# One load of matrices asked for a block later, and the first block of each hop closed six pairs later, in a seven-hop graph kernel

## The chip, the cores and the metric

The kernel runs on one core of a Trainium2 chip. The metric is the device time of one execution in microseconds. Three runs of the kernel before took 3917.54, 3921.28 and 3921.52 us; their median is 3921.28 us. The engines are named as in the profile: PE is TensorE's matmul pipe and PEld its weight loads, DVE is VectorE, ACT is ScalarE, POOL is GpSimd and SP is SyncE, which here only issues DMA. A suffix q (SPq, POOLq, ACTq) names the same engine's queue of DMA issues and waits.

## The reference

A graph of 10,000 nodes and 160,000 edges has a row of 128 numbers for each node. Seven times in a row each node's new row is the weighted sum of the rows of the nodes with an edge into it; the eight versions of a node (the input and seven hops) are then the tokens of a small attention block.

```python
h = x
toks = [x]
for _ in range(K):                                  # K = 7
    msg = h[src] * deg_inv_sqrt[src, None] * deg_inv_sqrt[dst, None]
    h = _segment_sum(msg, dst, N)
    toks.append(h)
tok = jnp.stack(toks, axis=1)                       # (N, K+1, D)
t = _layernorm(tok, axis=-1)
...
o = tok + jnp.einsum('nkd,de->nke', o, wo)
r = _layernorm(o, axis=-1)
alpha = _softmax(jnp.einsum('nkd,d->nk', r, w_r), axis=-1)
return jnp.einsum('nk,nkd->nd', alpha, o)
```

A hop needs all rows of the hop before it: an edge may come from any node. That is why the border between two hops, called a seam here, is a place where work can run dry.

## The kernel before, in words

The nodes are cut into 79 blocks of 128 rows; 78 of them go through the main path. A hop's rows are kept twice: as a table in SBUF (`tab`, fp16 in a high and a low half, so 256 columns) and as a table in DRAM (`tabd`, and its last seven blocks once more as `tabh`). Edges were sorted once, in the first stage, into 0/1 matrices (`gsd` in DRAM), 592 KB for each block of targets. In the hops 2 to 7 such a block, `block()`, does this:

- `gather(jj)`, nine times, one for each pair of edge groups: eight matmuls (L635) pick source rows out of the SBUF table into the PSUM tile `p` (six buffers), and ACT or DVE copies `p` to `eb` (L638; pairs with jj % 3 = 1 go to DVE). All 72 matmuls of a block's nine gathers stand in a row on PE.
- `begin()`: opens the accumulator `acc` (PSUM, two buffers) with rows that were fetched from DRAM by indirect DMA into `og`: one matmul for the rows from `tabh` (L599, `og,w`), and one for the overflow rows from `tabd` (L599, `og,Sov`).
- `scat(jj)`, nine times: two matmuls for each pair (L613) add the rows of `eb` into `acc`.
- `close()`: ends the sum. In the first two blocks of a hop (`late`) the overflow rows are added only here (L626), and not in `begin()`, because the DMA that fetches them must wait until the last rows of the hop before have been stored to `tabd`. Then `finish()` reduces `acc` to `s` on DVE (L585), `next_rows()` scales `s` into the next table (three DVE instructions, L665 to L667, in all hops but the last) and stores it to `tabd` (L162), and `token_out()` writes the hop's rows out (POOL L675, SP L677).

The list `pend` carries `scat` and `close` behind `gather`: after the nine gathers of a block, all but the last two entries of `pend` are run. So PE sees, for block n: 72 gather matmuls of n, `begin` of n, the last two pairs of n-1 (four matmuls), the `close` of n-1, and the first seven pairs of n (14 matmuls). At the end of a hop the list is emptied.

The overflow rows of the first five blocks of a hop are asked for by `over()`, issued on POOL from `ahead()`: for block 0 while block 0 gathers, for the blocks 1 and 2 while block 1 gathers, for 3 and 4 while block 2 gathers. Those issues are POOL's L559, each behind a small copy (L569) that ties it to a point of the gathers. In the seam of the hops 2 to 6, the scale of the next table is worked out as well (`scale`, a short chain of DVE and two tiny PE steps, L129 and L137).

The 0/1 matrices of a block come by a load on SP's queue (`load_w`, L760, tile `w`, five buffers): at each block the list `ws` of loaded blocks is filled up to four. A load waits until PE has done with the buffer that it reuses.

What sets the order: the code is written in the order told above, but a scheduler between the code and the chip places the instructions on each engine's queue. Where a line of code stands is therefore not where its instruction stands; the order of the built program is shown with the change. Each engine runs its own queue in order.

In names below, "block 0" is the first block that a hop works on (the blocks held in `tabh` go first), "block 1" the second, and T is the time at which the overflow rows of block 0 are there and PE goes on.

Of the kernel before, what the change touches and what calls it, by code (L numbers as in the profile page):

```python
# [40 lines left out]
class Hops:  # L41
    def __init__(self, ctx, dp, missing, tab1, tc, x, src, dst, dis):
# [68 lines left out]
        self.Sov = cp.tile([128, NW + NE, 128], F8, name="Sov")  # L111
        self.oidx = cp.tile([128, NW + NE, NI + 1], I32, name="oidx")
        self.ebuf = []
        self.eb_i = 0
        self.more_ebufs(cp, 5, True)

# [471 lines left out]
    def block(self, t, w, tab, og, pend, lag, runs, first, evac, fin, lead=False, late=False, mid=None, ahead=None):  # L588
# [8 lines left out]
        def fetched(i, start=False, stop=False):  # L597
            W = w[:, (NG + i) * 128:(NG + i + 1) * 128] if i < NI else self.Sov[:, t, :]
            T.matmul(acc[0][:, :256], W, og()[i], start=start, stop=stop)  # L599
            if first:  # L600
                T.matmul(acc[0][:, 256:257], W, self.ones16, start=False, stop=False)

        def begin():
            acc.append(self.pacc.tile([128, 512], F32, name="acc", tag="acc"))
            for i in range(NI if late else NI + 1):
                fetched(i, start=i == 0)
# [22 lines left out]
        def gather(jj):  # L629
            n = min(2, NG - 2 * jj)  # L630
            p = self.pg.tile([128, 2, 2, 128], F32, name="p")
            for j in range(n):
                for q in range(4):
                    s = 4 * (2 * jj + j) + q
                    T.matmul(p[32 * q:32 * q + 32, j], w[:, NJ * 128 + s * CAP:NJ * 128 + (s + 1) * CAP], tab[:, s, :], start=True, stop=True)  # L635
            e = self.ebuf[self.eb_i % len(self.ebuf)]
            self.eb_i += 1
            (A.copy if evac(jj) else V.tensor_copy)(e[:, :n, 0:256], p[:, :n].rearrange("p j h d -> p j (h d)"))  # L638
            pend.append(lambda: scat(e[:, :n], jj))

        jj = 0
        for i, n in enumerate(runs):
            for _ in range(n):
                gather(jj)
                if jj == 0 and not first:
                    ahead(self.ebuf[(self.eb_i - 1) % len(self.ebuf)][:, 0, 0:1])
                jj += 1
            if mid and not lead:
                mid(1)
            if not first:  # L650
                begin()
            while len(pend) > lag:
                pend.pop(0)()
            if mid and lead:
                mid(0)
            if i == len(runs) - 1:
                pend.append(close)
            yield

    def next_rows(self, t, s, new, c, mx, i, eng, queue=None):  # L660
# [18 lines left out]
    def run(self, ctx, beside, nhop=K):  # L679
        tc, nc, V, A, T, G = self.tc, self.nc, self.nc.vector, self.nc.scalar, self.nc.tensor, self.nc.gpsimd  # L680
        with ExitStack() as c:
# [11 lines left out]
            pend = []  # L693
# [46 lines left out]
        with ExitStack() as c:  # L740
# [10 lines left out]
            pend, ws = [], []  # L751
# [3 lines left out]
            def load_w():  # L755
                t = next(todo, None)
                w = None
                if t is not None:
                    w = self.gsp.tile([128, (NJ + NG) * 128], F8, name="w")
                    nc.sync.dma_start(w, self.GSd[t])  # L760
                ws.append(w)
# [3 lines left out]
            for k in range(2, nhop + 1):  # L765
# [39 lines left out]
                def ahead(n, after, k=k, pair=pair, over=over):  # L805
                    if n >= NW - 2:
                        for m in (0, 1) if n == NW - 2 else (2, 3):
                            if k < nhop:
                                pair(k + 1, m, after, False)
                    elif n == 0:  # L810
                        pair(k, 4, after, False)
                        over(k, 0, after)
                    elif n < 3:
                        for m in (2 * n - 1, 2 * n):
                            over(k, m, after)
                    else:
                        pair(k, n + 2, after)
                    if n in (8, 12, 16):
                        self.fetch_end(n // 4 - 2, dins[k % 2][0], after)
# [2 lines left out]
                    for m in range(4):  # L822
                        pair(k, m, None, False)
                for n, t in enumerate(order):
                    while len(ws) < 4:
                        load_w()
                    for _ in self.block(t, ws.pop(0), tab, lambda n=n, og=og: og[n], pend, 2, (9,), False, lambda jj: jj % 3 != 1, fin, n == 0, n < 2,
                                        scale if n < 2 and not last else None, lambda after, n=n: ahead(n, after)):
                        pass
                    beside(k, n, self.pg)  # L830
                    if n == 20:
                        pend.append(lambda fin=fin: self.end_block(False, fin))
# [556 lines left out]
```

## Time and profile before

| what | value |
|---|---|
| three runs, median | 3921.28 us (3917.54 to 3921.52) |
| profiled execution, its own time | 3918.07 us |
| span from its first to its last instruction | 3916.3 us |
| PE busy | 3652.7 us (93%) |
| DVE, ACT, POOL busy | 3150.7, 2686.2, 1776.1 us |
| mean granted TensorE clock | 0.974 |
| L626, `acc<-og,Sov`, idle of PE ahead of it | 18.8 us in five places |
| loads of matrices `w<-gsd` | 468 of 592 KB |
| issues of overflow and `tabh` rows `og` | 546 each |

The page of a profile counts instructions by line, engine and operation: L613 is line 613 of the kernel, whichever loop called it. A row of a timeline gives the start in us from the first instruction, the time until the last of the merged instructions ended, engine, line, operation, output and input tiles, shapes and count; in brackets stands how long the engine had been idle and what ended that. Matmuls are pipelined, so that the start of one to the start of the next is shorter than its duration. In a table of windows the columns are the stretch, its length, the busy time of the five engines with their counts, the granted clock of TensorE, the busy share of the DMA engines and GB/s. In the chain of work a row gives start, duration and what the end of the program hung on at that time.

The stages follow one another: sorting and hop 1 up to about 1136 us, the hops 2 to 7 from there to about 3235 us at roughly 349 us each, and the attention behind them. The seams ahead of the hops 2 to 7 lie at about 1143, 1490, 1839, 2187, 2536 and 2884 us.

### The profile page before, as it was taken

What the parts mean: (1) busy time and instruction counts of PE and PEld (TensorE: products, weight loads), DVE (VectorE), ACT (ScalarE), POOL (GpSimd) and SP (SyncE); (2) the same over time, 40 slices, a digit from 0 to 9 for tenths busy, and PEclk for the clock granted to TensorE, in tenths of its full rate; (3) what the DMA queues carried; (4) which work ended last, traced back from release to release, by engine and by line L of the source; (5) the groups of instructions that cost most, each with busy time, mean ns of one, the idle gap of its engine ahead of it and who ended that gap; (6) DMA issues with size and microseconds to landing.
All of it is one profiled execution on the core that took longest, in us unless ns stands there. A gap on an engine that the chain in (4) does not pass through costs nothing.

```text
span 3916.3 us, 165413 instructions
## 1 busy us (share of the span) xinstructions
PE 3652.7 (93%) x69041; PEld 2993.2 (76%) x69041; DVE 3150.7 (80%) x7033; ACT 2686.2 (69%) x6806; POOL 1776.1 (45%) x2409
## 2 busy tenths in 40 slices
PE   4776899999989999999999999999999999999996
PEld 3675666777668888888888888888888887888885
DVE  8999999999977777777777777777765556999998
ACT  6665455666666676666666666666666669888884
POOL 0000334333346666665666666666666662222222
PEclk8888999999999999999999999999999999999997
DMA  3100354554556666666666666666667551222220
GB/s 94 44 2 1 117 177 157 173 166 154 171 165 203 201 203 193 203 200 189 208 203 200 193 202 203 199 199 200 203 200 216 184 171 37 75 76 75 78 76 20
DMA packets 320871, 590.60 MB, mean 151 GB/s; under 512 B 56767, under 2 KB 214685, under 8 KB 314861
## 3 DMA queue, kind: packets, MB, share of 16 engines
q1 hardware_dynamic: 268829, 495.82, 40.8%
q0 software_dynamic: 35616, 73.01, 6.9%
q10 hardware_dynamic: 15664, 11.09, 1.0%
q8 instruction: 542, 8.88, 0.9%
q14 instruction: 220, 1.80, 0.1%
HBM read 451.66 MB, written 128.06 MB: 148 GB/s over the span
## 4 chain that ended last, share of the span: by engine, by line
PE 66%; DVE 2%; DMA 1%; ACT 1%; issue 1%; POOL 0%; ACTq 0%; POOLq 0%; DVEq 0%
PE p L635 24%; PE acc L613 23%; PE acc L599 4%; PE pv L1049 3%; PE po L1060 3%; PE pu L1038 3%; PE pt L1028 2%; PE ps L1080 1%; PE pf L1228 1%; PE sm L1086 1%; DMA og<-tabd,oidx 1%; ACT junk L1074 0%; DMA tabd<-tab 0%; DVE st L1155 0%; DVE o L1066 0%
## 5 line engine op out<-in xcount | busy, mean ns | idle before, releaser
L638 ACT CAST eb<-p 128x512 f16<-128x512 f32 x3494 | 1790.6, 600 | 784.9 <-PE p L635 769.9
L638 DVE CAST eb<-p 128x512 f16<-128x512 f32 x1420 | 948.2, 691 | 450.8 <-PE p L635 448.6
L635 PE MATMUL p<-tab,w 128*32 128x256 f16 x39312 | 1257.2, 274 | 13.5 <-DMA w<-gsd 4.7
L613 PE MATMUL acc<-eb,w 128*128 128x256 f16 (+1 forms) x9828 | 1238.9, 274 | 3.5 <-DVE eb L638 1.2
L635 PEld LDWEIGHTS <-w 128*32 128x32 fp8e4 x39312 | 986.8, 97 | 195.8 <-issue 143.3
L613 PEld LDWEIGHTS <-w 128*128 128x128 fp8e4 x9828 | 940.1, 98 | 178.3 <-issue 64.6
L559 POOL DMA_INDIRECT og<-tabh,oidx x546 | 597.0, 1093 | 705.9 <-DVE vi L444 395.1
L559 POOL DMA_INDIRECT og<-tabd,oidx x546 | 591.9, 1084 | 536.8 <-PE acc L626 322.7
L585 DVE TENSOR_REDUCE s<-acc 128x128 f32<-128x256 f32 x553 | 233.8, 423 | 133.3 <-PE acc L613 109.5
L675 POOL TENSOR_SCALAR r<-s,ctok 128x128 f32<-128x128 f32 x474 | 296.6, 626 | 37.0 <-DVE s L585 22.7
L319 ACT ACTIVATE o<-oh,d2s 128x79 f16<-128x79 f16 x800 | 204.6, 373 | 81.1 <-PE ta L333 81.1
L1074 ACT ACTIVATE junk<-tab 128x128 f32<-128x128 f32 x625 | 245.1, 394 | 0.1
L569 POOL COPY og<-eb 128x2 f16<-128x2 f16 (+1 forms) x494 | 91.8, 189 | 322.9 <-ACT eb L638 322.6
L1060 PEld LDWEIGHTS po<-v,pT 128*128 128x128 f32 x1250 | 158.9, 193 | 44.7 <-issue 27.4
L333 PE MATMUL ta<-o,ro 128*128 128x158 f16 x1250 | 119.9, 267 | 77.9 <-DVE ro L329 77.9
L1132 POOL TENSOR_TENSOR p<-e,in 128x512 f32<-128x512 f32 (+1 forms) x40 | 40.8, 1019 | 332.6 <-DVE e L1130 301.3
L666 DVE SCALAR_TENSOR_TENSOR tab<-s,c,tab 128x128 f16<-128x128 f32 x474 | 170.5, 360 | 15.0 <-ACT tab L663 1.0
L1049 PE MATMUL pv<-Wv,xT 128*128 128x131 f32 x1250 | 176.0, 284 | 4.8 <-ACT xT L1029 4.1
L333 PEld LDWEIGHTS <-ro 128*128 128x128 f16 x1250 | 114.7, 114 | 82.2 <-DVE ro L329 82.1
L1060 PE MATMUL po<-v,pT 128*128 128x128 f32 x1250 | 166.7, 277 | 7.7 <-DVE o L1066 7.7
L1049 PEld LDWEIGHTS pv<-Wv,xT 128*128 128x128 f32 x1250 | 153.3, 191 | 21.7 <-issue 8.2
L599 PE MATMUL acc<-og,w 128*128 128x256 f16 x546 | 154.0, 282 | 0.0
(310 smaller groups left out, 4537.1 us busy)
## 6 DMA issues: line engine op xcount, KB each, us to landing
w<-gsd SPq DMA_DIRECT2D x468, 592.0 KB
gsd<-w SPq DMA_DIRECT2D x78, 592.0 KB
rb<-srow SPq DMA_DIRECT2D x78, 576.0 KB
tok<-r SPq DMA_DIRECT2D x546, 64.0 KB
tab<-tok SPq DMA_DIRECT2D x273, 128.0 KB
tabd<-tab SPq DMA_DIRECT2D x390, 64.0 KB
og<-tabh,oidx POOLq DMA_INDIRECT x546
og<-tabd,oidx POOLq DMA_INDIRECT x546
```

The source lines that it names most:

```text
L319: A.activation(o[:, j - a, NK:, i], oh[:, j, :, i], AF.Copy, scale=d2s[:, c0:c0 + 1])
L333: T.matmul(ta, ro[:, j - a, :, i], o[:, j - a, :, i], start=j + i == 0, stop=j + i == NP)
L559: self.nc.gpsimd.indirect_dma_start(out=o, out_offset=None, in_=src[0] if i == NI else src[1], in_offset=bass.IndirectOffsetOnAxis(ap=self ...
L585: self.nc.vector.tensor_reduce(s, acc[:, 0:256].rearrange("p (h d) -> p d h", h=2), axis=X, op=ALU.add)
L599: T.matmul(acc[0][:, :256], W, og()[i], start=start, stop=stop)
L613: T.matmul(acc[0][:, :m], w[:, J * 128:(J + 1) * 128], e[:, j, :m], start=first and J == 0, stop=J == NG - 1 and not (first or late))
L635: T.matmul(p[32 * q:32 * q + 32, j], w[:, NJ * 128 + s * CAP:NJ * 128 + (s + 1) * CAP], tab[:, s, :], start=True, stop=True)
L638: (A.copy if evac(jj) else V.tensor_copy)(e[:, :n, 0:256], p[:, :n].rearrange("p j h d -> p j (h d)"))
L675: self.nc.gpsimd.tensor_scalar(r, s, ct[:, t:t + 1], None, op0=ALU.mult)
L1049: T.matmul(p[:, g - a, :], S[i]["xT"][:, g, :], Wv, start=True, stop=True)
L1060: T.matmul(p[:, g - a, :], PT[i % 2][:, g, :], S[i]["v"][:, g, :128], start=True, stop=True)
L1074: A.activation(j, S[i]["x"][:, g, :], AF.Square, bias=S[i]["x"][:, g, 0:1], scale=-1.0, accum_out=S[i]["sq"][:, g:g + 1])
```

## The change

Two edits in the code of the hops 2 to 7. The first: at block 0 of the hops 3 to 7 the list `ws` is filled to three and not to four, so that the load for block 3 is asked for in block 1's turn together with that for block 4. The second: the `close` of block 0 of each hop is not appended to `pend`; it is held and put into `pend` in block 1's turn behind the first six pairs of block 1. Nothing is computed differently, and no instruction is added or removed.

```diff
@@ Hops.__init__
         self.ebuf = []
+        self.held = []
         self.eb_i = 0
@@ Hops.block
             if not first:
                 begin()
+                if self.held:
+                    pend.insert(lag + 6, self.held.pop())
             while len(pend) > lag:
                 pend.pop(0)()
             if mid and lead:
                 mid(0)
             if i == len(runs) - 1:
-                pend.append(close)
+                (self.held if lead and not first else pend).append(close)
             yield
@@ Hops.run
                 for n, t in enumerate(order):
-                    while len(ws) < 4:
+                    while len(ws) < (3 if n == 0 and k > 2 else 4):
                         load_w()
```

What the built programs hold at the seam ahead of hop 3 follows; the other seams read alike. First PE, before: the last pair of block 0 (`eb_22475`), the close of block 0 (`og,Sov`), and the first pairs of block 1.

```order
L613 MATMUL acc<-eb_22475,w 128x256
L613 LDWEIGHTS w
L613 MATMUL acc<-eb_22475,w 128x256
L626 LDWEIGHTS Sov
L626 MATMUL acc<-og,Sov 128x256
L613 LDWEIGHTS w
L613 MATMUL acc<-eb_22476,w 128x256
L613 LDWEIGHTS w
L613 MATMUL acc<-eb_22476,w 128x256
L613 LDWEIGHTS w
L613 MATMUL acc<-eb_251,w 128x256
```

PE in the changed kernel, from the sixth pair of block 1 (`eb_259`) on: the close stands behind it, the seventh pair (`eb_22468`) follows, and then the gathers of block 2 begin (L636 here is L635 before).

```order
L614 MATMUL acc<-eb_259,w 128x256
L614 LDWEIGHTS w
L614 MATMUL acc<-eb_259,w 128x256
L627 LDWEIGHTS Sov
L627 MATMUL acc<-og,Sov 128x256
L614 LDWEIGHTS w
L614 MATMUL acc<-eb_22468,w 128x256
L614 LDWEIGHTS w
L614 MATMUL acc<-eb_22468,w 128x256
L636 LDWEIGHTS w
L636 MATMUL p<-tab_239,w 32x256
```

So twelve matmuls of block 1, with their weight loads, have moved from behind the close to ahead of it, in each of the hops 2 to 7. Second, SP's queue at the same seam, before; `gsd75`, `gsd76` and `gsd77` are the matrices of the blocks 3, 4 and 5 of hop 3, `tabd0` the rows of the last blocks of hop 2, `tok2` and `tok3` the written rows of the hops 2 and 3.

```order
L760 DMA w_32438<-gsd75_143 128x4736
L162 DMA tabd0_146<-tab0_239 128x256
L677 DMA tok2_151<-r_32407 128x128
L760 DMA w_32558<-gsd76_144 128x4736
L677 DMA tok2_151<-r_32434 128x128
L760 DMA w_32697<-gsd77_145 128x4736
L162 DMA tabd1_147<-tab1_64 128x256
L166 DMA tabh1_149<-tab1_64 128x256
L677 DMA tok3_152<-r_32680 128x128
L760 DMA w_32825<-gsd0_68 128x4736
```

SP's queue in the changed kernel:

```order
L763 DMA w_32556<-gsd75_143 128x4736
L163 DMA tabd0_146<-tab0_239 128x256
L680 DMA tok2_151<-r_32407 128x128
L763 DMA w_32558<-gsd76_144 128x4736
L680 DMA tok2_151<-r_32434 128x128
L763 DMA w_32697<-gsd77_145 128x4736
L680 DMA tok3_152<-r_32692 128x128
L163 DMA tabd1_147<-tab1_64 128x256
L167 DMA tabh1_149<-tab1_64 128x256
L763 DMA w_32825<-gsd0_68 128x4736
```

The load for block 3 (`gsd75`) has a new number and the same place, ahead of the rows of the next-to-last block; what has moved on SP is block 0's token store, from behind the two row stores of block 0 to ahead of them. The last block's own rows are stored from ACT's queue, which is the same in both programs, as is POOL's. Third, DVE: before, the reduction of block 0 stands ahead of the scale of the tokens, `ctok`.

```order
L781 TENSOR_TENSOR sinv_247<-sinv_247,q2_32659 128x1
L585 TENSOR_REDUCE s_32673<-acc_32535 128x128
L770 TENSOR_SCALAR ctok0_243<-disT_221,sinv_247 128x79
L665 TENSOR_SCALAR tab1_64<-s_32673,c11_246 128x128
L666 SCALAR_TENSOR_TENSOR tab1_64<-s_32673,c11_246,tab1_64 128x128
L667 TENSOR_REDUCE mx0_241<-tab1_64 128x1
L638 CAST eb9_22472<-p_32713 128x2x256
```

DVE in the changed kernel:

```order
L784 TENSOR_TENSOR sinv_247<-sinv_247,q2_32659 128x1
L773 TENSOR_SCALAR ctok0_243<-disT_221,sinv_247 128x79
L586 TENSOR_REDUCE s_32685<-acc_32533 128x128
L668 TENSOR_SCALAR tab1_64<-s_32685,c11_246 128x128
L669 SCALAR_TENSOR_TENSOR tab1_64<-s_32685,c11_246,tab1_64 128x128
L670 TENSOR_REDUCE mx0_241<-tab1_64 128x1
L639 CAST eb9_22472<-p_32713 128x2x256
```

The two have changed places; the copies of block 2's gathers (`eb9_22472` on) still stand behind block 0's reduction and its three rows of scaling.

## The prediction

> **What bounds the kernel now.** I read the page first, then the table of PE's waits, and then PE's timeline at each seam.
>
> ```profile
> span 3916.3 us, 165413 instructions
> PE 3652.7 (93%) x69041; PEld 2993.2 (76%) x69041; DVE 3150.7 (80%) x7033; ACT 2686.2 (69%) x6806; POOL 1776.1 (45%) x2409
> PE acc L626 <- DMA og<-tabd,oidx: 18.8, 5, 4.0
> ```
>
> PE sets the time, and within the hops the longest of its waits is the one that the change touches: the close of a hop's first block stands still for its overflow rows five times, 18.8 us in all. The timeline of PE at the seam ahead of hop 3, followed by block 1's close, which runs undisturbed:
>
> ```profile
> 1499.20 0.40 PE L626 MATMUL acc<-og,Sov 128*128 128x256 f16 x1 [3.96 <-DMA og<-tabd,oidx]
> 1499.39 3.19 PE L613 MATMUL acc<-eb,w 128*128 128x256 f16 x14
> 1502.52 3.16 PE L635 MATMUL p<-tab,w 128*32 128x256 f16 x72
> 1505.72 0.27 PE L599 MATMUL acc<-og,Sov 128*128 128x256 f16 x1
> 1506.27 0.27 PE L626 MATMUL acc<-og,Sov 128*128 128x256 f16 x1
> 1506.38 1.69 PE L613 MATMUL acc<-eb,w 128*128 128x256 f16 x14
> 1508.00 2.15 PE L635 MATMUL p<-tab,w 128*32 128x256 f16 x72
> 1510.20 0.27 PE L599 MATMUL acc<-og,Sov 128*128 128x256 f16 x1
> ```
>
> The stall is 3.96 us, and what follows is slow as well: 14 matmuls take 3.19 us where the same 14 later take 1.69, and 72 take 3.16 against 2.15. From the close to the next block's L599 with `Sov` it is 6.52 us here (1499.20 to 1505.72) and 3.93 us undisturbed (1506.27 to 1510.20): a tail of 2.59 us. The other four seams:
>
> ```profile
> 1848.03 0.39 PE L626 MATMUL acc<-og,Sov 128*128 128x256 f16 x1 [3.73 <-DMA og<-tabd,oidx]
> 1854.22 0.27 PE L599 MATMUL acc<-og,Sov 128*128 128x256 f16 x1
> 2196.30 0.40 PE L626 MATMUL acc<-og,Sov 128*128 128x256 f16 x1 [3.85 <-DMA og<-tabd,oidx]
> 2202.44 0.27 PE L599 MATMUL acc<-og,Sov 128*128 128x256 f16 x1
> 2545.04 0.28 PE L626 MATMUL acc<-og,Sov 128*128 128x256 f16 x1 [3.70 <-DMA og<-tabd,oidx]
> 2550.59 0.27 PE L599 MATMUL acc<-og,Sov 128*128 128x256 f16 x1
> 2891.91 0.40 PE L626 MATMUL acc<-og,Sov 128*128 128x256 f16 x1 [3.60 <-DMA og<-tabd,oidx]
> 2898.40 0.27 PE L599 MATMUL acc<-og,Sov 128*128 128x256 f16 x1
> ```
>
> Stalls of 3.96, 3.73, 3.85, 3.70 and 3.60 us, and distances of 6.52, 6.19, 6.14, 5.55 and 6.49 us, so tails of 2.59, 2.26, 2.21, 1.62 and 2.56 us. A seam costs about 6 us, all five 30 us. The seam ahead of hop 2 is another kind; there the close's rows come in time (no idle in PE's row), and the chain of work hangs on the third fetch, which block 2's L599 needs:
>
> ```profile
> 1151.61 0.27 PE L626 MATMUL acc<-og,Sov 128*128 128x256 f16 x1
> 1151.70 4.09 DMA og<-tabd,oidx
> ```
>
> The tail is the clock, as windows of 3.41 us show, which is the grid on which the granted clock changes in this trace (column behind POOL's):
>
> ```profile
> 1494.39:1497.80 3.41, 0.86 (x7) 0.53 (x7) 0.94 (x5) 1.16 (x3) 2.04 (x4) 1.00 0.45 150
> 1497.80:1501.21 3.41, 2.01 (x10) 1.45 (x11) 1.50 (x5) 0.00 (x0) 1.28 (x3) 0.50 0.27 73
> 1501.21:1504.63 3.42, 3.42 (x49) 2.21 (x51) 0.69 (x1) 1.12 (x3) 0.89 (x4) 0.50 0.29 79
> 1842.55:1845.96 3.41, 1.75 (x35) 1.13 (x23) 1.83 (x8) 2.05 (x5) 1.24 (x3) 1.00 0.20 51
> 1845.96:1849.37 3.41, 1.34 (x7) 0.97 (x8) 0.88 (x4) 0.00 (x0) 2.34 (x4) 0.50 0.59 191
> 712.73:716.14 3.41, 1.84 (x34) 1.22 (x33) 3.41 (x8) 1.97 (x4) 2.61 (x2) 1.00 0.17 38
> 716.14:719.55 3.41, 3.41 (x92) 2.82 (x90) 3.15 (x13) 2.01 (x6) 0.00 (x0) 1.00 0.25 63
> 2941.64:2945.05 3.41, 0.82 (x30) 0.58 (x22) 0.87 (x2) 1.78 (x4) 2.57 (x6) 1.00 0.93 286
> 2945.05:2948.46 3.41, 3.41 (x28) 2.19 (x17) 0.69 (x1) 0.58 (x1) 0.71 (x1) 0.50 0.85 202
> ```
>
> A window with PE busy 0.86 or 1.75 us is followed by half the clock, one with 1.84 us is not: some 1.65 us of idle in one window is enough. A half-clock window that is itself partly idle (2.01 us busy) is followed by another; a full one (3.41 us at 1501.21) is the last.
>
> **The change part by part.** *The load asked for later* costs and brings nothing by my reading: SP's queue shows it in its old place, and it issues there at 1486.22, ahead of the last rows' store on ACT's queue:
>
> ```profile
> 1486.22 0.32 SPq L760 DMA_DIRECT2D w<-gsd  x1
> 1489.91 4.66 DMA tabd<-tab
> 1495.60 3.56 DMA og<-tabd,oidx
> ```
>
> The last two rows are the chain of work: the store takes 4.66 us to land, then POOL issues the fetch for block 0, which lands 3.56 us later, and PE goes on. ACT's and POOL's queues are unchanged, so T, the moment of that landing, stays put against the work ahead of it. Were the load really behind the store, the bounds would be a gain of the store's whole 4.66 us per seam and a loss by a late matrix of block 3, which is gathered at 1508 or later, 20 us after the request: no loss. I take zero, as the queue's row is the nearest evidence.
>
> *The close six pairs later.* Twelve matmuls move from behind the stall to ahead of it. Their copies are older than they are, so they run at once: 15 steps from 1506.38 to 1508.00 give 0.108 us each, 1.30 us for twelve. As T stays, the stall shrinks by 1.30 us, to 2.66, 2.43, 2.55, 2.40 and 2.30 us. That is 6.5 us in five seams if the clock does afterwards what it does now.
>
> It should do better. At random phase against a 3.41 us grid, an idle of G puts at least 1.65 us into one window with a chance of G/3.41 + 0.03, so 0.82, 0.75, 0.78, 0.74 and 0.71; on average 0.76. The remainder in the next window is below about 1 us, mostly too little for a second half-clock window. One full one costs 3.41/2 = 1.71 us. With it a seam gains 1.30 + tail - 1.71: 2.18, 1.85, 1.80, 1.21, 2.15 us. Without it, 1.30 + tail: 3.89, 3.56, 3.51, 2.92, 3.86 us.
>
> *What is late next.* Two things stand close behind. The first is block 2's L599, which needs the third overflow fetch. POOL issues it here:
>
> ```profile
> 1500.08 0.97 POOL L559 DMA_INDIRECT og<-tabd,oidx  x1 [2.09 <-issue]
> 1847.41 0.95 POOL L559 DMA_INDIRECT og<-tabd,oidx  x1 [0.30 <-issue]
> 2196.50 0.94 POOL L559 DMA_INDIRECT og<-tabd,oidx  x1 [2.10 <-issue]
> 2544.37 0.94 POOL L559 DMA_INDIRECT og<-tabd,oidx  x1 [0.30 <-issue]
> 2893.09 0.94 POOL L559 DMA_INDIRECT og<-tabd,oidx  x1 [2.10 <-issue]
> ```
>
> With the 3.56 us of the first fetch they land at 1503.64, 1850.97, 2200.06, 2547.93 and 2896.65; L599 cannot pass these, which caps the gains at about 2.0, 3.2, 2.3, 2.6 and 1.7 us. The second is DVE, which scales block 0's rows before it copies for block 2:
>
> ```profile
> 1500.90 0.27 DVE L667 TENSOR_REDUCE mx<-tab 128x1 f32<-128x128 f16 x1
> L638 DVE CAST eb<-p 128x512 f16<-128x512 f32 x1420 | 948.2, 691 | 450.8 <-PE p L635 448.6
> ```
>
> The scaling is done 1.97 us after T, 1.8 with `ctok` ahead of it; the copy of block 2's second pair (0.69 us, the mean of its group on the page) is then done at T + 2.5. The eighth pair of a block reuses the PSUM buffer of the second. At full clock block 2 begins at T + 0.44 (four steps of 0.108) and reaches its eighth pair seven ninths of 2.15 us later, at T + 2.1, so it waits some 0.4 us: 3.5, 3.2, 3.1 and 2.5 us are left in the first four. At half the clock both are hidden. At hop 2's seam nothing is won, and the same DVE work, now 1.3 us later, stands in the way: from nothing to its whole 1.3 us; I take 0.3, as the next L599 there already waits for a fetch.
>
> POOL's `token_out` for block 0 still comes after that third fetch and ahead of those for blocks 3 and 4; since T stays, nothing behind it is later. SP's token store ahead of the row stores makes those wait for POOL's scaling; they are read a hop later, at no cost. The load behind them on SP (`gsd0`) needs block 1's buffer, which PE frees only after block 2's gathers.
>
> *The sum.* With half a clock in every seam: 2.0 + 1.85 + 1.8 + 1.2 + 1.7 = 8.6 us. Full clock: 2.0 + 3.2 + 2.3 + 2.5 + 1.7 = 11.7. Weighted 0.76 to 0.24: 9.3, less 0.3: 9.0 us. The profiled execution took 3918.07 us of its own (span 3916.3), which gives 3909; it lies 3.2 us under the median of 3921.28, from which it would be 3912. I say 3910.5.
>
> **The rivals.** *No half clock after the shorter stall.* For: the stalls fall to 2.3 to 2.7 us. Against: the window at 2941.64 holds 2.59 us of idle, and 0.50 follows. Price: 11.7 - 0.3 = 11.4 us, so 3908. The Trainium skill's page "TensorE: Matmul & The Clock Gate", in its section on HAM oscillation, puts the limit at gaps over about 3.4 us, by which every seam would stay at full clock. By that rule, the trace disagrees: 1.66 us of idle at 1842.55 was enough.
>
> *The clock tail stays as long as it is.* The twelve matmuls alone: 6.5 - 0.3 = 6.2 us, 3913.5. For: in four of five seams two half windows follow now. Against: the second comes where the window after the first is itself idle by 1.4 us or more, and 1 us is about the most that is left.
>
> *A second wait takes the first one's place (slower).* The third fetch lands late and PE stops at block 2's L599, idle once more. For: three of five issues already stand 2.1 us for nothing that the profile names. Against: POOL's order is the same. Were all five fetches later by 2.1 us, the caps would add up to 11.8 - 10.5 = 1.3 us; slower than before begins at 2.4 us in each seam, and 4 us make it 8 us slower: 3927.
>
> *The load does move.* Then the store lands earlier, T with it by up to 2 us of the 4.66, and the gain is up to 10 us more; the queue speaks against it, and I count it with the first rival.
>
> **How the numbers follow.** The forecast (half clock for one window in most seams, 8 to 10 us) has 0.50, its own range 3907 to 3914; no half clock 0.14; the tail as it is 0.20; the second wait 0.08; and 0.08 that pauses elsewhere, like the 2.59 us one at 2941.64, shift and eat or hide the gain. 0.2% (7.8 us), about what a measurement of this kernel can tell from none, lies inside the forecast's edge: of the first two cases I give 0.60 to faster; the tail as it is, the shifted pauses and that edge make 0.33 the same; slower 0.07. The range: 3903, the full-clock gain from the lower base with 3 us of the runs' spread, to 3917.5, where 4 us are won from the median.
>
> **What would show it.** Right: L626's line in PE's waits falls from 18.8 to about 12 us; it starts 2.3 to 2.7 us idle; the load at SP stands ahead of the rows' store; L599 with `Sov` follows L626 by 2.6 to 4.9 us. Wrong: a wait at L599 longer than 1.5 us, T moved against the row store's issue, or two half-clock windows in most seams.

## The result, and the profile after

The changed kernel takes 3909.74 us (median of 22 runs, 3902.24 to 3919.81), the kernel before in the same sitting 3919.48 us (22 runs, 3911.33 to 3926.99). The ratio is 0.9978 with a 95% interval of 0.9971 to 0.9985: 0.22% faster, which is 8.6 us of the 3919.48. The edits shift the line numbers: L626 of before is now L627, L599 is L600, L613 is L614, L635 is L636, and the load L760 is L763.

The profiled execution is a long one, 3918.95 us. From its page and from the table of PE's waits:

```profile
span 3917.2 us, 165414 instructions
...
PE acc L627 <- DMA og<-tabd,oidx: 14.4, 5, 4.0
```

The first block's closes still wait five times, 14.4 us against 18.8. The span is no shorter than before, but the time lies elsewhere: the hops 2 to 7 begin at 1147.95 us here and at 1138.27 before, since sorting and hop 1, which the change does not touch, took 9.7 us more in this execution. The hops 2 to 7 took 2089.38 us against 2097.76, 8.4 us less; what lies behind them took the same (679.8 and 680.3 us).

PE's timeline at the five seams (start, duration, engine, line, and in brackets the idle time):

```profile
1504.91 1.91 PE L614 MATMUL acc<-eb,w 128*128 128x256 f16 x16
1509.82 0.39 PE L627 MATMUL acc<-og,Sov 128*128 128x256 f16 x1 [3.00 <-DMA og<-tabd,oidx]
...
1510.57 4.03 PE L636 MATMUL p<-tab,w 128*32 128x256 f16 x72
1514.72 0.42 PE L600 MATMUL acc<-og,Sov 128*128 128x256 f16 x1
...
1859.09 0.28 PE L627 MATMUL acc<-og,Sov 128*128 128x256 f16 x1 [3.98 <-DMA og<-tabd,oidx]
1862.80 0.42 PE L600 MATMUL acc<-og,Sov 128*128 128x256 f16 x1
...
2205.33 0.40 PE L627 MATMUL acc<-og,Sov 128*128 128x256 f16 x1 [2.46 <-DMA og<-tabd,oidx]
2209.51 0.27 PE L600 MATMUL acc<-og,Sov 128*128 128x256 f16 x1
...
2552.14 0.28 PE L627 MATMUL acc<-og,Sov 128*128 128x256 f16 x1 [2.43 <-DMA og<-tabd,oidx]
2555.99 0.42 PE L600 MATMUL acc<-og,Sov 128*128 128x256 f16 x1
...
2897.98 0.29 PE L627 MATMUL acc<-og,Sov 128*128 128x256 f16 x1 [2.56 <-DMA og<-tabd,oidx]
2902.23 0.27 PE L600 MATMUL acc<-og,Sov 128*128 128x256 f16 x1
```

Sixteen matmuls (x16, four of block 0 and the twelve of block 1) now stand ahead of the close, and two behind it. The close waits 3.00, 3.98, 2.46, 2.43 and 2.56 us. At no L600 does a bracket appear: the third fetch is always in time. The gathers behind the first close take 4.03 us, nearly twice the 2.15 us of full clock. Windows on the 3.41 us grid show why (the granted clock is the column behind POOL's):

```profile
1505.50:1508.91 3.41, 1.32 (x13) 0.93 (x10) 0.41 (x3) 0.31 (x1) 2.17 (x4) 1.00 0.63 210
1508.91:1512.32 3.41, 2.50 (x39) 1.59 (x43) 1.89 (x5) 0.76 (x2) 1.88 (x4) 0.50 0.13 32
1512.32:1515.74 3.42, 3.42 (x50) 2.23 (x43) 1.49 (x3) 2.56 (x5) 1.97 (x2) 0.50 0.41 88
...
1853.65:1857.07 3.42, 1.45 (x14) 1.06 (x11) 0.52 (x4) 0.44 (x1) 2.41 (x5) 1.00 0.59 190
1857.07:1860.48 3.41, 1.39 (x39) 1.16 (x43) 1.00 (x4) 0.51 (x2) 1.32 (x2) 1.00 0.19 49
...
2201.81:2205.22 3.41, 1.06 (x10) 0.70 (x8) 0.23 (x1) 0.06 (x1) 2.21 (x4) 1.00 0.62 205
2205.22:2208.63 3.41, 3.30 (x55) 2.17 (x59) 2.05 (x6) 1.56 (x3) 1.95 (x5) 0.50 0.13 31
```

All five seams still drop to half the clock. In the first the window after the stall is itself idle for 0.91 us (2.50 busy), and a second half-clock window follows; in the others one is the last. At the second seam the grid cuts the stall of 3.98 us into two idle pieces of 1.97 and 2.02 us: the clock stayed full behind the first window (1853.65) and fell to half only behind the second, at 1860.48. So the prediction's "some 1.65 us of idle in one window is enough" is no sharp limit: 1.66 us were enough at 1842.55 in the kernel before, 1.97 were not here. The chain of work, with the store of the last rows and the fetch for block 0:

```profile
1500.18 4.20 DMA tabd<-tab
1505.40 4.37 DMA og<-tabd,oidx
...
1848.46 4.96 DMA tabd<-tab
1854.19 4.85 DMA og<-tabd,oidx
...
2889.28 1.78 DMA tabd<-tab
2891.96 5.97 DMA og<-tabd,oidx
```

The fetch took 4.85 us at the second of these seams and 5.97 at the last, where the fetches of before took 3.3 to 4.2.

**A ledger for the hops.** Between two seams a block takes 4.37 us, as two of its opening rows in the kernel before show, 1702.95 and 1707.32. What a seam costs can then be counted from the opening of a hop's last block but one to that of the next hop's seventh block, less eight such periods. For the seam ahead of hop 3, before:

```profile
1480.99 0.28 PE L599 MATMUL acc<-og,w 128*128 128x256 f16 x1
...
1523.18 0.28 PE L599 MATMUL acc<-og,w 128*128 128x256 f16 x1
...
1702.95 0.28 PE L599 MATMUL acc<-og,w 128*128 128x256 f16 x1
...
1707.32 0.28 PE L599 MATMUL acc<-og,w 128*128 128x256 f16 x1
```

and after:

```profile
1491.26 0.28 PE L600 MATMUL acc<-og,w 128*128 128x256 f16 x1
...
1532.68 0.28 PE L600 MATMUL acc<-og,w 128*128 128x256 f16 x1
```

That is 42.19 us before and 41.42 after, less 34.94 (eight periods of 4.368): 7.25 and 6.48 us. All places, worked out in the same way; hop 2's start is counted from the end of hop 1 to its seventh block (six periods off), the rest of hop 7 from its seventh block to its last but one (70 off):

| place | before | after | gain |
|---|---|---|---|
| seam ahead of hop 3 | 7.25 | 6.48 | 0.77 |
| seam ahead of hop 4 | 6.69 | 6.32 | 0.37 |
| seam ahead of hop 5 | 6.87 | 4.83 | 2.04 |
| seam ahead of hop 6 | 6.03 | 4.76 | 1.27 |
| seam ahead of hop 7 | 6.36 | 4.39 | 1.97 |
| start of hop 2 | 9.16 | 9.73 | -0.57 |
| the rest of hop 7 | 5.13 | 2.61 | 2.52 |

The seams give 6.4 us. The 2.5 us of the last row belong to no seam: the pause of 2.59 us at 2941 us, in the middle of hop 7, which the prediction's windows showed with a half-clock window behind it, is shorter here and keeps the clock:

```profile
2947.34 0.61 PE L636 MATMUL p<-tab,w 128*32 128x256 f16 x14 [1.27 <-issue]
```

The table adds up to 8.37 us, the 8.4 us of the stage; what lies between these places took the same in both.

### The profile page after: what moved, and what is told of

Same layout as the page of the kernel before. It is cut to its first block, busy times and chain, and to the rows that moved or that the text cites. A ratio compares the mean times of both kernels' runs of the same rounds, so it can differ in the third digit from the quotient of the medians.

```text
span 3917.2 us, 165414 instructions
## 1 busy us (share of the span) xinstructions
PE 3658.1 (93%) x69041; PEld 3000.1 (77%) x69041; DVE 3151.5 (80%) x7033; ACT 2687.4 (69%) x6806; POOL 1772.8 (45%) x2409
## 4 chain that ended last, share of the span: by engine, by line
PE 75%; DVE 16%; DMA 5%; issue 1%; ACT 1%; SPq 0%; ACTq 0%; POOL 0%; DVEq 0%; POOLq 0%
PE p L636 26%; PE acc L614 24%; PE acc L600 4%; PE pv L1052 3%; DMA rb<-srow 3%; PE po L1063 3%; PE pu L1041 3%; PE ta L334 2%; DVE oh L200 2%; PE pt L1031 2%; DVE w L549 2%; DVE ro L330 1%; DVE ux L213 1%; DVE R L206 1%; DVE o L206 1%
## 5 line engine op out<-in xcount | busy, mean ns | idle before, releaser
L636 PE MATMUL p<-tab,w 128*32 128x256 f16 x39312 | 1260.3, 275 | 11.8 <-DMA w<-gsd 4.7
L614 PE MATMUL acc<-eb,w 128*128 128x256 f16 (+1 forms) x9828 | 1233.7, 274 | 3.4 <-DVE eb L639 1.2
L636 PEld LDWEIGHTS <-w 128*32 128x32 fp8e4 x39312 | 989.0, 97 | 194.1 <-issue 139.6
L614 PEld LDWEIGHTS <-w 128*128 128x128 fp8e4 x9828 | 937.3, 98 | 176.2 <-issue 65.1
L600 PE MATMUL acc<-og,w 128*128 128x256 f16 x546 | 154.2, 283 | 0.0
```

What stands on the lines that cost most here:

```text
L614: T.matmul(acc[0][:, :m], w[:, J * 128:(J + 1) * 128], e[:, j, :m], start=first and J == 0, stop=J == NG - 1 and not (first or late))
```

## The experiments

The first eight runs were made on chips where the kernel before takes 4087 to 4088 us, the last four on chips where it takes 3919 to 3921 us. Each ratio compares with the kernel before on its own chip. Line numbers are those of the changed kernel; in the kernels that add lines the load is L765.

### One edit at a time

Only the close is moved, the load stays as it was:

```diff
-                    while len(ws) < (3 if n == 0 and k > 2 else 4):
+                    while len(ws) < 4:
```

> The second edit alone: block 0's close behind six pairs of block 1, the list of loads filled to four as before. Theory A, that the load edit moves nothing on any queue: the same time as the full change, 8 to 10 us under the kernel before, with stalls of 2.3 to 3 us at the closes of the hops 3 to 7. Theory B, that the later request frees the path of the last rows' store: less gain than the full change by whatever the load is worth, with stalls longer by that amount.

Measured: 4080.51 against 4088.35 us, ratio 0.9975 (0.9966 to 0.9985). In the traces the hops 2 to 7 of this run and of the full change hold the same instructions in the same order on every queue.

Only the load is asked for later:

```diff
-                (self.held if lead and not first else pend).append(close)
+                pend.append(close)
```

> The first edit alone: the load for block 3 is asked for a block later, the close stays where it was. Theory A, that the load's place on SP's queue does not change: the same time as the kernel before within 2 us, stalls of 3.6 to 4 us at the closes of the hops 3 to 7 on a chip like the first one. Theory B: 2 us or more under the kernel before, with shorter stalls.

Measured: 4086.78 against 4086.69 us, ratio 1.0004 (0.9995 to 1.0012). In the traces its hops 2 to 7 are those of the kernel before, instruction for instruction on every queue. So the whole gain is the close's, and the first edit never reached the chip: the scheduler puts the load back where it was. This run also serves as the trace of the kernel before on the slower chips.

### How much of it is the number of pairs

The close stands behind three pairs and not six:

```diff
-                    pend.insert(lag + 6, self.held.pop())
+                    pend.insert(lag + 3, self.held.pop())
```

> Full change, but the close is put behind three pairs of block 1 and not six. Theory A, that matmuls moved ahead of the stall count one by one and the clock drops whenever 1.65 us of idle fall into one window: six matmuls are 0.65 us a seam, stalls of 3.0 to 3.4 us, half the clock in at least four of five seams, 4 to 6 us under the kernel before. Theory C, that only six pairs are enough to escape the second half-clock window: 3.2 us under before and no more, tails as long as before (11 us in five seams).

Measured: 4083.67 us, ratio 0.9985 (0.9976 to 0.9994). From its table of waits:

```profile
PE acc L627 <- DMA og<-tabd,oidx: 14.6, 5, 3.8
```

No pair, three pairs and six pairs give 1.0004, 0.9985 and 0.9975 on these chips. Three pairs bring some 6 us and six some 10, which is 0.3 to 0.4 us of each of the five seams for a pair, and 0.22 us of it is its two matmuls at 0.108. The gain grows with the pairs; the intervals of three and six overlap, so nothing finer can be read. In this run's trace half the clock follows in four of the five seams, as theory A had it; theory C's 3.2 us lies within the interval, too, so the time alone does not exclude it.

### The clock's part

Twenty matmuls of table rows, whose results nobody reads, are put ahead of the held close, so that PE is not idle:

```diff
-                    pend.insert(lag + 6, self.held.pop())
+                    held = self.held.pop()
+                    def warm():
+                        z = self.pg.tile([128, 2, 2, 128], F32, name="z", tag="p")
+                        for _ in range(20):
+                            T.matmul(z[:, 0], self.id16, tab[:, 0, :], start=True, stop=True)
+                        held()
+                    pend.insert(lag + 6, warm)
```

> Full change, and ahead of the held close twenty matmuls of table rows into a spare PSUM tile that nobody reads (an addition; 20 x 0.108 = 2.2 us of work in the place of idle time). Theory A, that the tail behind a stall is the granted clock: 0.2 to 0.8 us idle at the close, clock 1.00 through all seams, from the close to the next block's matmul with Sov 2.6 to 3.0 us where the third fetch has landed and up to 4.4 where it has not; 11 to 14 us under the kernel before, so 2 to 5 us better than the full change. Rival D, that the slow matmuls after a stall come from the stall itself and not from the clock's window (operands or weights that arrive late): the rows behind the close stay slow and the time is that of the full change.

Measured: 4079.34 us, ratio 0.9975 (0.9966 to 0.9985). The same kernel once more:

> Twenty matmuls into a spare PSUM tile ahead of the held close, a second time, for a chip on which PE alone sets the hops. Theory A, that the tail is the granted clock: 0.2 to 0.8 us idle at the close, no half-clock window in the seams of the hops 3 to 7, 2 to 5 us under the full change. Rival D: rows behind the close as slow as in the full change.

Measured: 4078.11 us, ratio 0.9982 (0.9972 to 0.9992). PE's timeline at the seam ahead of hop 3 in this second run:

```profile
1538.76 2.35 PE L659 MATMUL z<-tab,id 128*128 128x256 f16 x20
1542.13 0.28 PE L627 MATMUL acc<-og,Sov 128*128 128x256 f16 x1 [1.02 <-DMA og<-tabd,oidx]
...
1542.56 1.71 PE L636 MATMUL p<-tab,w 128*32 128x256 f16 x56
```

(The second expectation was written for a faster chip; the run was on a slower one again.) At the seams ahead of the hops 3 to 7 the fill does what it is for. The 56 gathers behind the close run at full pace (1.71 us), and the five seams have no half-clock window in this run and one in the first, against three with the close alone (two from 1542.12 on, one at 2675.35). So the slow rows are the clock's, as theory A had it; but the time is that of the close alone, and not theory A's 2 to 5 us less. Two things go against the fill. It stands ahead of the close at the start of hop 2 as well, where the close alone has no wait:

```profile
1162.95 2.35 PE L659 MATMUL z<-tab,id 128*128 128x256 f16 x20
1165.13 0.27 PE L627 MATMUL acc<-og,Sov 128*128 128x256 f16 x1
```

By the ledger the start of hop 2 costs 13.15 us in the first run and 13.78 in the second, and 11.08 with the close alone: 2.1 and 2.7 us are lost there. And in the five seams the fill (20 matmuls at 0.109, so 2.2 us each) and the rest of the wait (4.3 us in all in the first run, 3.1 in the second) are together 3.2 and 2.0 us longer than the 12.0 us of waits that they replace. Even so the five seams cost 34.3 and 32.1 us, against 34.7 with the close alone. What lies behind the closes has therefore become 3.6 and 4.6 us shorter, with two and three half-clock windows fewer: 1.8 and 1.5 us for a window. From the load alone to the close alone it is less, 2.3 us for four windows, in which part of the stall itself had lain. One execution of each is traced, so these are rough; the equal times do not show that the clock costs nothing, since the fill spends elsewhere what it wins. A fill at the five seams alone was not tried, nor any fill on the faster chips.

### The load really behind the store

Into the buffer of each of the loads for the blocks 3 and 4 one element of block 0's last pair is copied first, on ACT. The load must wait for that copy, which the scheduler cannot pull ahead:

```diff
             def load_w(after=None):
...
+                    if after is not None:
+                        A.copy(w[:, 0:2].bitcast(F16), after)
                     nc.sync.dma_start(w, self.GSd[t])
...
-                        load_w()
+                        load_w(self.ebuf[(self.eb_i - 1) % len(self.ebuf)][:, 0, 0:1] if n == 1 and k > 2 else None)
```

> Full change, and the loads for the blocks 3 and 4 of the hops 3 to 7 are really held until ACT has copied block 0's last pair (a one-element copy into the load's tile, overwritten by the load), so that they issue some 2 us behind the last rows' store. Theory F, that the loads in flight stretch the store: the store lands in 2.3 to 3 us and not 4 to 5, T comes 1 to 2 us earlier, 5 to 10 us under the full change. Rival G, that the loads then stretch the fetch in the store's place, or that one slow DMA engine and not the amount in flight sets the landing: store faster, fetch slower, T within 0.5 us of where it was, the time of the full change within 2 us.

Measured: 4071.73 against 4086.69 us, ratio 0.9965 (0.9953 to 0.9977). The chain at the seam ahead of hop 3 in the kernel before on such a chip, and in this one:

```profile
1523.13 5.43 DMA tabd<-tab
...
1529.58 2.86 DMA og<-tabd,oidx
```

```profile
1525.19 2.93 DMA tabd<-tab
...
1529.20 0.95 POOL L560 DMA_INDIRECT og<-tabd,oidx  x1 [3.02 <-issue]
...
1532.87 0.28 PE L627 MATMUL acc<-og,Sov 128*128 128x256 f16 x1 [1.03 <-DMA og<-tabd,oidx]
```

(The chain no longer runs through the fetch for block 0 here; its issue on POOL and the close that waits for it are shown instead.) The store lands 2.5 us sooner once the 592 KB loads for the blocks 3 and 4 do not start ahead of it. The Trainium skill's page "DMA: Bandwidth & Descriptors", section "Latency and other measured facts", says that the memory's answer, and with it the fixed cost of a transfer, is quicker when its load is lighter; the trace agrees in direction, 2.93 against 5.43 us. But the fetch has become longer: from its issue to the close it is 3.67 us (1529.20 to 1532.87), where it was 2.91 (1529.58 to 1532.49). Two loads start as the store ends (L765, from 1527.45) and run beside it, and a third follows 4.6 us later. So both came, the quicker store of theory F and the slower fetch of rival G. Which of them has the time right was not settled: 0.9965 here and 0.9975 for the close alone have overlapping intervals.

The late loads with the close in its old place, on a faster chip:

> The kernel before, with the loads for the blocks 3 and 4 held behind the last rows' store by a one-element copy, and the close in its old place. Theory F (the store's landing sets T, and a 592 KB load that runs beside it stretches that landing): the store lands some 2.5 us earlier than in the kernel before on the same chip (2.9 instead of 5.4 us at hop 3's seam, as in e6), so the closes' stalls of 3.5 to 4.0 us fall to 1.2 to 1.9 us, at most two of the five seams still have a half-clock window, and the seven seconds' worth of seams gain 2.2 us each plus the tail: 8 to 14 us, ratio 0.9965 to 0.998. If the gains of the two edits are one and the same (either alone takes the clock tail away, and both together little more): 10 us, and e6's 15 us less this is under 6 us. Rival (the loads cost nothing by themselves, e6's gain came from the moved close on a good run): ratio 0.9995 to 1.0005, stalls of 3.5 to 4.0 us. Rival (matrices come late): PE waits at L636 for the load in block 3, ratio above 1.000.

(The "seven seconds' worth of seams" stands for the five seams.) Measured: 3913.5 against 3919.41 us, ratio 0.9987 (0.9979 to 0.9996), about 5 us. The stalls are 2.41 and 2.34 us in two seams, and 4.11, 4.12 and 5.33 in the others. The fetches for block 0 in the chain at two of these:

```profile
2189.55 5.88 DMA og<-tabd,oidx
...
2884.58 7.68 DMA og<-tabd,oidx
```

Here the loads run beside the fetch for block 0 instead of the store, and that takes 5.88 and 7.68 us. Half the clock follows in four seams, not in two at most. So the forecast of 8 to 14 us fell: what the store wins, the fetch loses in three seams of five.

Both edits, the close behind six pairs and the loads late, on a faster chip:

> The kernel of e6 (full change and the loads for the blocks 3 and 4 held behind the store) once more, beside its sister below on one chip. If the chip is the one on which the kernel before takes some 3919 us: gains add up (close alone 8.5, late loads alone 5 us), 12 to 16 us, ratio 0.996 to 0.997, and the step to the close behind block 2's gathers is worth the other 8 to 12 us of the 25 in e10. Rival (the late loads only pay together with the early close: the store is then free and no idle is left to spoil the clock): 0.9945 to 0.9955, the same as e10 within its interval.

Measured: 3907.41 against 3920.53 us, ratio 0.9967 (0.9955 to 0.998), some 13 us. That is the sum of the two parts (8.6 and 5 us) within the intervals, as the first case had it. The rival that puts it level with the close in block 2, 0.9945 to 0.9955, touches the interval only at its edge.

### The close into block 2

The close of block 0, and the last two pairs and the close of block 1, are put behind the gathers of block 2, and the blocks 0 to 3 take their overflow rows at their close. The loads stay in their old place:

```diff
+            if self.held and due:
+                self.held.pop()()
+                for _ in range(3):
+                    pend.pop(0)()
             if not first:
                 begin()
-                if self.held:
-                    pend.insert(lag + 6, self.held.pop())
...
-  ... fin, n == 0, n < 2, ...
+  ... fin, n == 0, n < 4, ..., n == 2):
```

> Block 0's close held until block 2's gathers are done, directly ahead of block 1's last two pairs, its close and block 2's begin; the overflow rows of the blocks 2 and 3 are added at their closes too, as for the blocks 0 and 1. Theory A, that the wait for the fetches and the clock are all that a seam costs: stalls under 0.6 us in every seam, no half-clock window, 24 to 29 us under the kernel before. Rival E, that the second and third fetches, DVE's scaling or the PSUM accumulators become the next wait: 10 to 18 us under before, with PE idle ahead of block 1's close or of block 2's accumulator.

Measured: 4079.68 us, ratio 0.9978 (0.9969 to 0.9987). Once more:

> The close of block 0 held until block 2's gathers are done, the blocks 0 to 3 closed late, a second time, for a chip on which PE alone sets the hops. Theory A: stalls under 0.6 us in every seam, no half-clock window, 20 to 29 us under the kernel before. Rival E: some 10 us under before as on the slower chip, with PE idle ahead of block 2's accumulator or waiting for DVE's copies.

Measured: 4079.82 us, ratio 0.998 (0.9972 to 0.9989). (Again a slower chip, not the faster one of the expectation.) The waits at the close have all but gone here (one of 1.0 us is left), and yet it is no faster than the close behind six pairs. PE's timeline shows what came in their place, at the seam ahead of hop 4:

```profile
1914.73 1.87 PE L636 MATMUL p<-tab,w 128*32 128x256 f16 x48
1916.97 0.32 PE L636 MATMUL p<-tab,w 128*32 128x256 f16 x4 [0.38 <-issue]
1917.71 0.35 PE L636 MATMUL p<-tab,w 128*32 128x256 f16 x4 [0.42 <-issue]
```

After two thirds of block 2's gathers PE stops for 0.4 us behind every four or so, six times, and the profile names nothing that it waits for; the window is then idle enough for half the clock. Rival E is what came, another wait in the place of the first, and the gain of 8 to 9 us is even below its 10 to 18. Then the same kernel on a faster chip:

> The kernel of e4 and e8 (close behind block 2's gathers, loads in their old place) once more. If the gain of e10 is the sum of its parts: 25 less the 5 of the late loads, so 18 to 20 us on the chip where the kernel before takes 3919 us, ratio 0.995 to 0.9955. Rival (as in e4 and e8, DVE is late instead): 0.9975 to 0.9985, and the two edits pay only together. On the slower chip the second rival's ratio is expected again.

Measured: 3896.43 against 3920.53 us, ratio 0.9941 (0.9927 to 0.9954), 23 us. The rival that the two edits pay only together fell; of the sum's 0.995 to 0.9955 the better end lies in the interval. PE's timeline at the seams ahead of hops 3 and 5:

```profile
1500.99 2.15 PE L636 MATMUL p<-tab,w 128*32 128x256 f16 x72
1503.89 0.28 PE L627 MATMUL acc<-og,Sov 128*128 128x256 f16 x1 [0.75 <-DMA og<-tabd,oidx]
1505.49 0.28 PE L627 MATMUL acc<-og,Sov 128*128 128x256 f16 x1 [0.88 <-DMA og<-tabd,oidx]
...
2189.65 2.15 PE L636 MATMUL p<-tab,w 128*32 128x256 f16 x72
2191.94 0.28 PE L627 MATMUL acc<-og,Sov 128*128 128x256 f16 x1
2192.50 0.27 PE L627 MATMUL acc<-og,Sov 128*128 128x256 f16 x1
```

Block 2's 72 gathers need no row of the last blocks' store, so 2.15 us more of work cover the same wait: two short idles of 0.75 and 0.88 us at the first seam, none at the second. One half-clock window is left in the five seams, at 2878.84, behind a stall of 2.33 us. In the ledger the five seams cost 2.64, 2.76, 1.09, 1.14 and 4.24 us, 11.9 against 33.2 before: 21.3 us of the 23.

With the loads late as well:

> The full change with the loads for the blocks 3 and 4 held behind the store, and the close of block 0 put behind the gathers of block 2 (the blocks 0 to 3 take their overflow rows at their close). Theory F: e6 had 1.0 and 1.6 us of idle left at closes and 1.3 and 1.2 us at block 2's L600; with the close in block 2 these four waits of 5.1 us and the last half-clock window (1.7 us) go, so the hops 2 to 7 take about 2239 us against e6's 2244.6 and the ratio is 0.995 to 0.9965. Rival (DVE becomes what is late: block 0's reduction and scaling, now two blocks after their rows, stand among the copies of block 2 or 3, as in e4 and e8): waits of 0.4 to 1.1 us at L636 take the place of those removed, no more than e6: ratio 0.9965 to 0.9975. Rival (the seam is already spent; what is left in the hops is DVE's steady pace): hops 2243 to 2246 us, ratio 0.9965.

Measured: 3894.33 against 3919.41 us, ratio 0.9942 (0.993 to 0.9955), some 23 us. The seams cost 10.8 us in the ledger. The times expected were for the slower chips; as a ratio it is better than any case had it, as is the kernel without the late loads. This ratio and that one's, 0.9941, can't be told apart: with the wait covered, an earlier store buys nothing that these runs can measure. Both are faster than the changed kernel and than the kernel before; the version without late loads is the simpler one.

## Why the prediction came out, point by point

The forecast was 3910.5 us, the median is 3909.74. The sum behind it was 9.0 us, the interval of the ratio is 5.9 to 11.4 us. The number was right; its parts were right only in some places.

**The load.** "Costs and brings nothing by my reading": right, and shown. SP's queue after has the load for block 3 ahead of the store's start at 1500.18, 3.7 us as before:

```profile
1496.48 0.32 SPq L763 DMA_DIRECT2D w<-gsd  x1
```

and alone it gives a ratio of 1.0004. The rival that the load does move fell. What the prediction said of a load really behind the store, a gain of up to 4.66 us a seam, was too generous: the store was some 2.5 us quicker, the loads then slowed the fetch, and 5 us were left over all five seams.

**Twelve matmuls ahead of the stall.** Right in kind: 16 matmuls in 1.91 us stand ahead of the close, and three stalls, 2.46, 2.43 and 2.56 us, are the 2.55, 2.40 and 2.30 of the forecast within 0.3 us. The step that failed is "as T stays". From the issue of the last rows' store on ACT's queue to the close it was 9.29, 9.07, 9.19, 9.04 and 8.43 us before (1489.91 to 1499.20 and so on); after it is 9.64, 10.63, 9.10, 9.07 and 8.70 (1500.18 to 1509.82 and so on). T stayed at the seams ahead of the hops 5 and 6 and moved at the other three, which was one of the prediction's signs of being wrong; the L627 line is 14.4 us, not about 12.

The second seam lost 1.56 us to a fetch of 4.85 us, where it had been 3.27. The loads there start as long ahead of the fetch as before, and the traces of the close alone and of the three pairs have 9.59 and 8.92 us at this place, so that much of this differs from one execution to another. The last seam is different. In the traces of the full change, of the close alone and of the three pairs the first load beside the store starts 0.34 to 0.53 us behind it, in the kernel before and in the load alone 0.01 us. The store then lands in 1.57 to 1.78 us, against 4.23 and 3.65, and the fetch takes 5.97 to 6.28 us, against 3.26 and 3.73: the trade of the late loads above, with a loss of 0.3 to 0.6 us in place of a gain. Why the load starts later there was not followed up. The forecast's range had no term for either.

**The clock.** Half a clock in most seams was right, in all five in fact, though the limit of 1.65 us from which its chance of 0.76 was worked out is not sharp, as the second seam shows. The term was mis-sized at two points. The remainder in the next window, "mostly too little for a second half-clock window", was 0.91 us at hop 3 and enough. And the tail was measured as far as block 2's opening, L599; but the close now stands nearer to it, so that part of the slow stretch lies behind it, where the measure does not look. In the ledger block 2's own period, from its opening to the next, is 5.05, 5.09, 4.59 and 4.95 us in the first four seams after, and 4.48, 4.48, 4.59 and 4.48 before. Seam by seam the sum had 2.0, 1.85, 1.8, 1.2 and 1.7 us, and the ledger has 0.77, 0.37, 2.04, 1.27 and 1.97 us: three terms held within 0.3 us, the first failed by the second slow window, the second by the late fetch. The seams gave 6.4 us, not 8.6 or more.

The rival without half a clock fell, and with it, for this kernel, the rule of the Trainium skill's page "TensorE: Matmul & The Clock Gate" (section on HAM oscillation) that only gaps above about 3.4 us cost the clock: a stall of 2.46 us, 2.35 of idle in one window, was followed by 0.50. The rival with the tail as long as before held in one seam of five, hop 3's, with two slow windows before and after (hop 6 had one before and has one after, as the sum took it). That the tail is worth its windows in time, 1.71 us for a full one, was assumed; on the slower chips the fill gives 1.8 and 1.5 us for a window, and the step from the load alone to the close alone 0.6.

**What is late next.** The third fetch's cap was never reached: no L600 waits, because no seam won more than 2.04 us. The slower case, a second wait there, did not come. That DVE's work is hidden under half the clock was not contradicted. At hop 2, 0.3 us of loss was taken, and 0.57 were lost.

**What made the number good.** The pause in the middle of hop 7 gave 2.5 us that the sum did not have; the prediction had it as a risk of 0.08, in either direction. In this pair of traces, 6.4 - 0.6 + 2.5 = 8.4 us. Whether the 22 runs owe as much to that pause can't be read, as one execution of each is traced; in other traces of the faster chips the block at that place takes 0.5 to 2.4 us too long, with whatever edit. The median's 8.6 us may thus hold more than the seams, or the seams may give more in other executions. The one other pair of traces speaks for the second: on the slower chips the same two programs, the load alone and the close alone, have five seams of 43.7 and 34.7 us, a gain of 9.0. This stays open.

## What to carry to other kernels

A wait at a border is best covered by work that does not need what is waited for: six pairs (1.3 us) won 0.2%, and one block's gathers more (2.15 us), with the late rows added behind them, 0.6% on the same kind of chip. An edit of the code that is meant to move a transfer has to be looked for in the order of the built program; here it was undone, and when it was forced, the loads hindered the next transfer and 5 us were left. A tail of a stall is counted up to where the pace is again the old one, not up to the next landmark that the change itself moves.

## What the runs showed of the hardware

- A half-clock window holds on to its half with less idle than it takes to lose the full clock: 0.91 us of idle in a half-clock window of 3.41 us kept it down (1508.91), 0.11 us did not (2205.22). From full clock 1.66 us of idle in a window were once enough (1842.55 before) and 1.97 us once not (1853.65 after), so the limit lies near there without being sharp in these figures.
- The store of the last rows, 64 KB, took 2.93 us to land with the 592 KB loads for the blocks 3 and 4 behind it and 5.43 us with them ahead of it (seam ahead of hop 3); an indirect fetch took 2.86 to 7.68 us, the longest with two loads beside it.
- The same built program takes 3919 us on some chips and 4087 us on others, all of the difference in the hops 2 to 7 (2097.76 and 2259.7 us; what lies behind them takes 680 us on both). On the slower chips DVE stands idle for longer ahead of its reduction (1.74 us in the row below, 0.20 at the same place on the faster chip), and PE then waits for DVE's copies, 169 times in the run of the load alone and once in the changed kernel's trace:

```profile
1705.19 0.42 DVE L586 TENSOR_REDUCE s<-acc 128x128 f32<-128x256 f32 x1 [1.74 <-remote]
```

```profile
PE p L636 <- DVE eb L639: 65.7, 169, 0.7
```

The first row is of a timeline, the second of the waits. What makes the difference wasn't found; it decides what an edit is worth, 0.2% or 0.6% for the close in block 2.
- In three of the five seams POOL still stands 2.09 us ahead of its third fetch for nothing that the profile names, in the kernel before, after the change and, on the faster chip, with the close in block 2 alike.
